# Two attentions on one core: output products one step later at the block boundary

## The chip, the cores and the metric

The kernel runs on one core of a Trainium2 chip. The metric is the device time of one execution in microseconds (us), median of several runs. Engines are named as in the profile: PE is the TensorE matmul stream and PEld its weight loads, DVE is VectorE, ACT is ScalarE, POOL is GpSimd, and SP is SyncE, whose queue issues nearly all DMAs of the main loop. L898 means line 898 of the kernel.

## The reference

Two independent multi-head attentions run over inputs of 2048 positions and 576 features, with 32 heads of 18 features. Their results stand side by side in the output.

```python
# A: local, dilated: each position looks at 8 positions, 2 apart, behind it
qkv = (x @ wqkv).reshape(B, S, 3, H, Dh).transpose(2, 0, 3, 1, 4)
logits = einsum("bhsd,bhswd->bhsw", q, kg) * Dh ** -0.5     # kg, vg: the 8 gathered keys, values
o_a = einsum("bhsw,bhswd->bhsd", softmax(masked logits), vg)
a = o_a.transpose(0, 2, 1, 3).reshape(B, S, D) @ wo_A
# B: full attention, all 2048 keys for each query
o_b = einsum("bhqk,bhkd->bhqd", softmax(q @ k^T * Dh ** -0.5), v)
b = o_b.transpose(0, 2, 1, 3).reshape(B, S, D) @ wo_B
out = concatenate([a, b], axis=-1)
```

## The kernel before

**Order.** After the projections (about the first 416 us) there is one main loop of 512 steps. It works on B: 8 groups of 4 heads, 4 blocks of 512 queries in each group, 16 key tiles of 128 keys in each block. So step s belongs to block s // 16 and key tile kt = s % 16, and a "block" below is one group with one block of queries. A step computes the scores of its key tile for four heads on PE (`score`, L388), takes their exponentials on ACT (L398 for one head, L401 for two at once), and then multiplies the exponentials of the step before it with the values, which accumulates in the PSUM tile `po` (`weigh`, L898). The values are therefore one step late: step 16n (kt = 0) holds the last value product of the block before, the one that ends it, and step 16n + 1 (kt = 1) holds the first one of the next block. When a block ends, `finish` lets DVE copy `po` to `o` (L908), and only then may the next block's first value product overwrite `po`.

**Maxima.** The softmax of B needs a bound for each query before its scores. PE computes trial products of queries and keys (L239) and DVE takes their maxima (L256, L258, L272) some blocks ahead. How many stand in a step is the planner's `many`: 3 as a rule, 2 in a kt = 1 step unless the step before it holds output products (L1388). When a block's maxima are complete, DVE reduces them once more (L282) and transposes them (L290).

**A.** Attention A runs beside the loop in eight parts j = 0 to 7, each started 55 steps after the one before (`local`, L1014). POOL does most of it; DVE takes maxima (L1059) and ACT the exponentials (L1069). A part's result goes through DRAM (`dao`), comes back in tiles `at` and `ahl` (`get`, L1118 and L1120; one buffer each), and is multiplied with `wo_A` on PE. These are the output products: for each of a part's two row tiles there are two products of 288 columns, and each takes 27 matmuls of about 0.29 us in two queues, one on each half of PE's rows, which run side by side (L1239). ACT copies the one half's sum to `y` (L1138), DVE adds the other half's (L1142).

**Where a product stands.** The list `TURNS` (L56) holds the steps in which an output product may stand. `local` takes the next two free turns for each row tile, puts them in the set `producing`, plans the tile's `get` up to 9 steps ahead of the first, and plans the store of the finished rows 5 steps after the second:

```python
TURNS = sorted({NT * n + AT for n in range(1, 30)} | {A_FROM + GAP * j + 35 for j in range(NJ)} | set(MORE))
one = next(t for t in TURNS if t >= at + 7)
two = next(t for t in TURNS if t > one + 1)
pieces.append((max(at + 1, one - 9) - start, lambda n=n: get(n)))
```

A step with products carries two maxima more than `many`, uses seven PSUM banks as one pool instead of five and a pair, and PE's order in it is made by `in_turn` (L1245) from estimated times: the two queues alternate as their estimates say, and a bank is taken when DVE or ACT is expected to have emptied it. Other steps with three maxima follow the fixed order `PLAIN`.

**Queues.** Everything a step does beside this is called at its end from an agenda. The agenda gives the order in which an engine receives instructions, not a time: SP runs ahead of PE wherever nothing it must wait for stands in front. In SP's order stand, one step after a block's end, the store of the denominators (`den`, L932, which must wait for the copy `o`), and at the start of each group the loads of the queries and keys of the group two ahead (`qs`, `ks` from `dqk`, L215 and L216; twelve loads over six steps from the group's second step on), into one of three sets of tiles, which is free when the last scores that read it are done.

Of the kernel before, what the change touches and what calls it, by code (L numbers as in the profile page):

```python
# [40 lines left out]
EARLY_PAIRS = EARLY * NB * PIECES + 8  # L41
AHEAD = 7

AT = 0

MORE = (439, 441, 451, 467, 475, 477, 484, 486)

# [7 lines left out]

TURNS = sorted({NT * n + AT for n in range(1, 30)} | {A_FROM + GAP * j + 35 for j in range(NJ)} | set(MORE))  # L56

# [12 lines left out]
def two_attentions(ctx: ExitStack, tc, xa, wa, woa, xb, wb, wob, out):  # L70
# [45 lines left out]
    def pooled(apart_):  # L116

        nonlocal ring
        ring = "pool"
        n = 7 if apart_ else 5  # L120
        if apart_:
            pair_room()
            freed[5] = freed[6] = freed["pair"]
        rings.update({k: list(range(n)) for k in ("pool", "scores", "else")})

    def apart():

        nonlocal ring
        ring = "else"
        assert not held  # L130
        if len(rings["else"]) == 7:
            pair_room()
            freed["pair"] = max(freed[5], freed[6])
        n = sorted(range(5), key=lambda i: freed[i])
        rings["scores"] = [n[1], n[3]]
        rings["else"] = [n[0], n[2], n[4]]
# [44 lines left out]
    step = 0  # L181
# [8 lines left out]
    def due():  # L190
        for f in agenda.pop(step, []):
            f()
# [126 lines left out]
    given = [0, 0]  # L319
    projecting = True  # L320

    def maximum(r):

        given[r] += 1
        return blocks[find(lambda rest: rest[r])][1](r)
# [14 lines left out]
    def first_part(r):  # L340

        for i in range(2):
            given[i] += 0.5
        if open_parts:
            part, args = open_parts.pop()
        else:
            rest, _, part = blocks[find(lambda rest: rest[0] and rest[1] and rest[0][-1][0] > 1)]
            piece = rest[0].pop()
            assert rest[1].pop() == piece
            args = (0, *piece)  # L350
            open_parts.append((part, (1, *piece)))
        ps = bank()
        ins, _ = part(*args, r, ps)
        taken = rings[ring][-1]

        def second():
            if ring == "else":
                rings["else"].remove(taken)
                rings["else"].append(taken)
            return part(*args, 1 - r, ps, ins)[1]  # L360

        return second
# [7 lines left out]
    def score(g, b, kt, h, kind):  # L370

        assert (g, b) in placed
        qs, ks = sets[g % 3]
        p, r = divmod(h, 2)
        at = slice(64 * r, 64 * r + 56)
        if len(scored) == 4:
            scored.clear()
            counted[0] += 1
        parity = counted[0] % 2
        n = sum(k == kind for k in scored)  # L380
        scored.append(kind)
        if kind == "pair":
            if n == 0:
                both_scores[:] = [pair_of_banks()]
            ps = both_scores[0][:, 512 * n : 512 * n + 512]
        else:
            ps = bank("else" if projecting else "scores")
        nc.tensor.matmul(ps, ks[at, p, 128 * kt : 128 * kt + 128], qs[at, b, p], start=True, stop=True)  # L388
        filled(r, 226, ps if kind != "pair" else None if n else both_scores[0])
        if kind == "single":  # L390
            e = whole = (work if parity else e_room).tile([128, 512], F32, name=f"e{n}{parity}", bufs=1)
        else:
            if n == 0:
                both_es[:] = [e_room.tile([128, 1024], F32, name=f"ee{parity}", bufs=1)]
            whole = both_es[0]
            e = whole[:, 512 * n : 512 * n + 512]
        if kind != "pair":
            nc.scalar.activation(e, ps, AF.Exp, scale=SCALE)  # L398
            emptied("ACT", 490, r, ps)
        elif n:  # L400
            nc.scalar.activation(whole, both_scores[0], AF.Exp, scale=SCALE)  # L401
            emptied("ACT", 916, r, both_scores[0])
        return e
# [102 lines left out]
    def do_all(fs):  # L506
        for f in fs:
            f()
# [6 lines left out]
    with (tc.tile_pool(name="x", bufs=1, side="right") as xp,  # L515
# [367 lines left out]
        step = 0  # L883
# [106 lines left out]
    producing = set()  # L990
# [254 lines left out]
    def in_turn(queues):  # L1245

        while any(queues):
            at = []
            for r, q in enumerate(queues):
                need = q[0][0] if q else None  # L1250
                free = 0
                if need == "E":
                    free = parted_at[0]
                elif need == "pair":
                    free = 0 if "pair" in held else freed["pair"] + 165
                elif need:
                    free = min(freed[i] for i in rings[ring] if i not in held) + 165 if any(i not in held for i in rings[ring]) else 1e9
                at.append(max(busy[r], free) if q else 2e9)
            r = int(at[1] < at[0])
            busy[0], busy[1] = max(busy[0], at[r]), max(busy[1], at[r])  # L1260
            queues[r].pop(0)[1]()
# [109 lines left out]
    total = early + rest  # L1371

    def behind():

        most = 0
        for n in range(int(sum(given)) // (2 * PIECES), NG * NB):
            until = NT * n - AHEAD
            more = 3 * (until - step) + 2 * sum(step <= p < until for p in producing)
            most = max(most, 2 * PIECES * (n + 1) - int(sum(given)) - more)
        return most  # L1380
# [4 lines left out]
    while step < ALL:  # L1385
        n, kt = divmod(step, NT)
        g, b = divmod(n, NB)
        many = min(4 if behind() > 0 else 2 if kt == 1 and step > 1 and step - 1 not in producing else 3, total - int(sum(given)))  # L1388
        if open_parts and total - int(sum(given)) < 3:
            many = 1  # L1390
        es = [None] * 4
        products = inside.pop(0)() if inside else ([], [])
        plain = many == 3 and not any(products)
        if not plain:
            pooled(any(products))
        parts = many == 3 or many == 1 and open_parts
        left = many - parts
        a = left // 2 if left != 1 or given[0] >= given[1] else 1
        b_ = left - a
        extra = any(products) and int(sum(given)) + many + 2 <= total  # L1400
        ops = {"D": lambda: parted.append(first_part(0)) or parted_at.insert(0, busy[0] + 250), "E": lambda: parted.pop()()(),
               "A": lambda: maximum(0)(), "B": lambda: maximum(1)(),
               "+": lambda: None,
               **{c: lambda h=i % 4, kind="single" if i < 4 else "apart" if any(products) else "pair": es.__setitem__(h, score(g, b, kt, h, kind))
                  for i, c in enumerate("0123wxyz")}}

        def queue(text, own):
            q = []
            for c in text:
                if c == "+":  # L1410
                    q += own
                    own = []
                elif c == "p":
                    q += own[:1]
                    own = own[1:]
                else:
                    q.append((c if c == "E" else "pair" if c in "wxyz" and not any(products) else True, ops[c]))
            return q

        if plain:  # L1420
            do_all(ops[c] for c in PLAIN)
        elif any(products):
            in_turn([queue(ROWS[0].replace("D", "D" * parts).replace("A", "A" * min(a, 1)).replace("X", "A" * extra), products[0]),
                     queue(ROWS[1].replace("E", "E" * parts).replace("B", "B" * min(b_, 1)).replace("X", "B" * extra), products[1])])
        else:
            in_turn([queue("D" * parts + "0y" + "A" * a, []), queue("x" + "E" * parts + "B" * b_ + "3", [])])
        for fs in (behind_scores, outside):
            while fs:
                fs.pop(0)()

        if not plain and not paired and int(sum(given)) < total:
            apart()
        paired = paired or kt % 2 == 0 and int(sum(given)) == total
        for _ in range(1 if paired and step < ALL - 2 else len(waiting)):
            if waiting:
                waiting.pop(0)()
        if ready and (kt % 2 == 0 or not paired):
            weigh(ready.pop(0))
        ready.append((g, b, kt, es))
        if paired and kt % 2:  # L1440
            weigh(*ready)
            ready.clear()
        due()

        if len(waiting) > (0 if not paired else 2 if kt % 2 else len(waiting)):
            waiting.pop(0)()
        step += 1
# [24 lines left out]
```

## Time and profile before

| | |
|---|---|
| runs shown | 1588.29, 1587.92, 1584.57 us; median 1587.92 us |
| profiled execution | 1584.54 us, span 1582.7 us |
| granted TensorE clock | 0.999 |
| PE busy | 1571.9 us, 99% of the span |
| DVE busy | 1399.5 us, 88% |
| ACT busy | 1183.0 us, 75% |
| POOL busy | 966.0 us, 61% |

A window row of the profile gives a stretch's start and end, its length, and each engine's busy time in it with the number of instructions. The chain of work that ended last is given in order of time: start, length, and what ran. A row of the timeline gives start, length, engine, line, operation and how many instructions are merged in it. A step is bounded here by the end of its last value product (L898); "x8" in the chain is one step's value products.

### The profile page before, as it was taken

The page shows a single profiled execution, that of the slowest core. Times are in us where ns is not written, and L with a number is a line of the kernel's source. Part 1 is how long each engine was busy: PE and PEld are TensorE (multiplying, and loading weights), DVE is VectorE, ACT ScalarE, POOL GpSimd, SP SyncE. Part 2 cuts the span into 40 slices and gives each one's busy share as a digit, 9 for nine tenths or more (in the row PEclk, how much of TensorE's full clock was granted, in tenths as well). Part 3 has the DMA queues.
Part 4 walks back from the last instruction along what each step waited for, and adds up shares of the span by engine and source line. Part 5 has one row for each costly group of instructions (what it writes and reads, how often), then busy time and mean ns, then how long its engine had stood idle before and what let it go on. Part 6 is the DMA issues. An engine that isn't in the chain of part 4 may idle for free.

```text
span 1582.7 us, 34698 instructions
## 1 busy us (share of the span) xinstructions
PE 1571.9 (99%) x13400; PEld 949.5 (60%) x13400; DVE 1399.5 (88%) x2381; ACT 1183.0 (75%) x1916; POOL 966.0 (61%) x820
## 2 busy tenths in 40 slices
PE   9999999999999999999999999999999999999998
PEld 7999998888544444454444445444444445455776
DVE  5299999999999999999999999999999999999433
ACT  7323441211799999999998999999999999998444
POOL 2305752201267997994995995995995997940100
PEclk9999999999999999999999999999999999999999
DMA  8848964523322253253236225423613232234211
GB/s 260 222 130 210 260 183 123 161 81 93 75 56 55 64 114 95 65 139 104 58 85 170 58 67 142 96 54 105 141 56 92 67 86 79 62 124 158 85 39 61
DMA packets 190149, 173.12 MB, mean 109 GB/s; under 512 B 123120, under 2 KB 136944, under 8 KB 188256
## 3 DMA queue, kind: packets, MB, share of 16 engines
q1 hardware_dynamic: 185120, 159.36, 36.4%
q0 software_dynamic: 4032, 10.63, 3.2%
q8 instruction: 105, 1.72, 0.5%
q10 hardware_dynamic: 832, 0.92, 0.2%
q14 instruction: 60, 0.49, 0.1%
HBM read 97.47 MB, written 72.95 MB: 108 GB/s over the span
## 4 chain that ended last, share of the span: by engine, by line
PE 93%; DVE 2%; DMA 2%; issue 1%; POOL 1%; ACT 1%; SPq 0%; POOLq 0%; ACTq 0%; DVEq 0%
PE po L898 30%; PE bank L239 20%; PE bank L498 14%; PE bank L388 9%; PE bank L1239 8%; PE pair L388 7%; PE bank L424 4%; DVE mx L256 1%; DMA ks<-dqk 1%; POOL xlo L546 1%; DMA qs<-dqk 0%; DMA at<-dao 0%; DVE mx L272 0%; DVE o L908 0%; PE bank L664 0%
## 5 line engine op out<-in xcount | busy, mean ns | idle before, releaser
L239 PE MATMUL bank<-ks,qs 54*128 54x256 f32 (+1 forms) x2526 | 756.1, 373 | 1.2 <-DVE mx L256 0.5
L256 DVE TENSOR_REDUCE mx<-bank 128x1 f32<-128x512 f32 x1024 | 680.3, 684 | 60.7 <-PE bank L239 36.2
L239 PEld LDWEIGHTS bank<-ks,qs 54*128 54x128 f32 x2526 | 414.9, 184 | 427.5 <-DVE mx L272 308.3
L398 ACT ACTIVATE e<-bank 128x512 f32<-128x512 f32 x1024 | 610.9, 602 | 75.5 <-PE bank L388 68.6
L898 PE MATMUL po<-ee,v 128*19 128x512 f32 x2048 | 536.9, 599 | 1.0 <-DVE o L908 0.2
L898 PE MATMUL po<-e,v 128*19 128x512 f32 x2048 | 531.5, 599 | 0.0
L401 ACT ACTIVATE ee<-pair 128x1024 f32<-128x1024 f32 x478 | 487.5, 1020 | 0.3
L388 PE MATMUL bank<-qs,ks 56*128 56x512 f32 x1092 | 461.1, 442 | 0.0
L258 DVE TENSOR_REDUCE mx<-bank 128x2 f32<-128x512 f32 x546 | 356.1, 685 | 19.1 <-PE bank L239 6.9
L272 DVE TENSOR_REDUCE mx<-bank 128x2 f32<-128x512 f32 x478 | 326.1, 682 | 0.0
L388 PE MATMUL pair<-qs,ks 56*128 56x512 f32 x956 | 248.5, 396 | 0.0
L388 PEld LDWEIGHTS bank<-qs,ks 56*128 56x128 f32 x1092 | 194.6, 184 | 15.4 <-ACT e L398 8.3
L1090 POOL TENSOR_TENSOR pr<-lg,akv 128x1024 f32<-128x1024 f32 x72 | 157.0, 2201 | 0.6
L840 ACT ACTIVATE ohi<-bank 128x512 f32<-128x512 f32 (+1 forms) x56 | 30.6, 595 | 148.6 <-issue 126.3
L388 PEld LDWEIGHTS pair<-qs,ks 56*128 56x128 f32 x956 | 138.3, 186 | 0.0
L898 PEld LDWEIGHTS po<-ee,v 128*19 128x19 f32 x2048 | 69.8, 97 | 111.3 <-issue 107.4
L498 PE MATMUL bank<-xhi,ahi 64*128 64x512 f32 x448 | 114.6, 391 | 0.2 <-ACT ohi L843 0.2
L498 PE MATMUL bank<-xlo,ahi 64*128 64x512 f32 (+1 forms) x448 | 102.7, 392 | 0.2 <-POOL xlo L546 0.2
L498 PE MATMUL bank<-xhi,alo 64*128 64x512 f32 x416 | 101.0, 391 | 0.0
L1042 POOL TENSOR_TENSOR pr<-aq,akv 128x1024 f32<-128x1024 f32 x40 | 87.8, 2200 | 17.2 <-PE bank L239 16.0
L1092 POOL TENSOR_TENSOR pr<-pr 128x512 f32<-128x512 f32 x72 | 91.2, 1289 | 0.6
L652 POOL TENSOR_TENSOR olo<-olo,ohi 128x512 fp32r<-128x512 f32 x36 | 46.1, 1294 | 65.7 <-ACT ohi L651 61.3
(210 smaller groups left out, 2346.2 us busy)
## 6 DMA issues: line engine op xcount, KB each, us to landing
do<-n SPq DMA_DIRECT2D x28, 512.0 KB
da<-ohi SPq DMA_DIRECT2D x52, 256.0 KB
akv<-da SPq DMA_DIRECT2D x64, 175.5 KB
out<-y SPq DMA_DIRECT2D x32, 288.0 KB
qs<-dqk SPq DMA_DIRECT2D x30, 288.0 KB
ks<-dqk SPq DMA_DIRECT2D x30, 288.0 KB
at<-dao SPq DMA_DIRECT2D x64, 128.0 KB
rec<-drec SPq DMA_DIRECT2D x29, 256.0 KB
```

What stands on the lines that cost most here:

```text
L239: return nc.tensor.matmul(ps, qs[rows_, b, p, 128 * t : 128 * t + 128], ks[rows_, p, 512 * k + at : 512 * k + at + n], start=True, stop=True)
L256: nc.vector.tensor_reduce(mx[:, r, p, t, k : k + 1], ps, axis=AX.X, op=ALU.max)
L258: nc.vector.tensor_reduce(mx[:, r, p, t, 2 * k - 2 : 2 * k], ps.rearrange("q (h n) -> q h n", h=2), axis=AX.X, op=ALU.max)
L272: nc.vector.tensor_reduce(mx[:, :, p, t, 2 * k - 2 + i], ps.rearrange("q (h n) -> q h n", h=2), axis=AX.X, op=ALU.max)
L388: nc.tensor.matmul(ps, ks[at, p, 128 * kt : 128 * kt + 128], qs[at, b, p], start=True, stop=True)
L398: nc.scalar.activation(e, ps, AF.Exp, scale=SCALE)
L401: nc.scalar.activation(whole, both_scores[0], AF.Exp, scale=SCALE)
L498: nc.tensor.matmul(ps, a, b, start=start, stop=stop)
L898: nc.tensor.matmul(po[32 * i : 32 * i + 19], vs[g][:, kt, 19 * i : 19 * i + 19], es[i], start=kt == 0, stop=kt == NT - 1)
L1090: nc.gpsimd.tensor_mul(at, ap(st["lg"], (0, 2), (SUB, W), (1, SUB)), window(st["v"], n))
L1092: nc.gpsimd.tensor_add(at[:, :, :4], at[:, :, :4], at[:, :, 4:])
L1239: nc.tensor.matmul(sums_[r], a, b, start=i == 0, stop=i == len(both[r]) - 1)
```

## The change

```diff
-AT = 0
+AT = 1
...
-        many = min(4 if behind() > 0 else 2 if kt == 1 and step > 1 and step - 1 not in producing else 3, total - int(sum(given)))
+        many = min(4 if behind() > 0 else 2 if kt == 1 and step > 1 and step not in producing and step - 1 not in producing else 3, total - int(sum(given)))
```

The regular turns move from steps 16n to steps 16n + 1: from the step with the value product that ends a block to the step with the next block's first one. The second edit keeps three maxima in a kt = 1 step that holds a product. The other turns (45 + 55j and `MORE`) stay. Worked through the lines quoted above, the 32 steps with products of A are

```
before: 112 128 144 155 | 176 192 208 210 | 224 240 256 265 | 288 304 320 336
        352 368 375 384 | 400 416 430 432 | 448 451 464 467 | 475 477 484 486
after:  113 129 145 155 | 177 193 209 225 | 241 257 265 273 | 289 305 320 337
        353 369 385 401 | 417 430 439 441 | 449 451 465 467 | 475 477 484 486
```

with a part's four products between the bars. The step of a `get` moves with its product: for example from 199 to 200 (product 208, now 209), from 247 to 258 (product 256, now 265), and from 439 to 442 (product 448, now 449). Where a part's own step 45 + 55j holds no product, its exponentials are issued in two halves rather than one: that holds for steps 45 and 100 before, and for 210 and 375 as well after.

## The prediction

> **What bounds the kernel now.** I read the page first, then the chain of work that ended last, then windows over single steps.
>
> ```profile
> span 1582.7 us, 34698 instructions
> PE 1571.9 (99%) x13400; PEld 949.5 (60%) x13400; DVE 1399.5 (88%) x2381; ACT 1183.0 (75%) x1916; POOL 966.0 (61%) x820
> PE 93%; DVE 2%; DMA 2%; issue 1%; POOL 1%; ACT 1%; SPq 0%; POOLq 0%; ACTq 0%; DVEq 0%
> ```
>
> PE holds 93% of the chain: the matmuls bound the kernel, and the change neither adds nor removes one. So it can only alter how long PE waits. Thirteen plain steps in a row (275 to 287) give the length of a step in which nothing waits:
>
> ```profile
> 997.83:1023.90 26.07, 26.07 (x210) 11.50 (x210) 24.64 (x41) 26.00 (x40) 25.99 (x26) 1.00 0.46 107
> ```
>
> 26.07 / 13 = 2.005 us. Now the chain across a boundary whose kt = 0 step has products (288, then 289 and 290), and one without products (272, 273, 274):
>
> ```profile
> 1022.90 0.99 PE po L898 x8
> ...
> 1024.69 0.80 PE bank L1239 x12
> ...
> 1026.76 0.23 PE bank L388 x2
> 1026.99 0.98 PE po L898 x8
> ...
> 1028.99 0.98 PE po L898 x8
> ...
> 1031.30 0.98 PE po L898 x8
> ```
>
> ```profile
> 993.52 0.60 DVE mx L256
> 994.11 0.61 DVE o L908
> ```
>
> The value products of steps 287 to 290 start 4.09, 2.00 and 2.31 us apart: the product step is clean, kt = 1 is clean, and kt = 2 is 0.3 us too long. Without products kt = 1 itself is late: PE waits for the copy `o`, and the copy waited for the maximum in front of it. Over the run (first the windows of kt = 2 after the 19 boundaries with a product at kt = 0, 208 and 320 left out, then kt = 1 at the nine boundaries without one, each row the sum over its windows):
>
> ```profile
> sum 41.24, PE 41.24 PEld 19.36 DVE 41.16 ACT 41.18 POOL 34.00; mean PE 2.17 PEld 1.02 DVE 2.17 ACT 2.17 POOL 1.79
> sum 19.61, PE 18.62 PEld 7.63 DVE 19.61 ACT 19.59 POOL 12.97; mean PE 2.07 PEld 0.85 DVE 2.18 ACT 2.18 POOL 1.44
> ```
>
> 41.24 - 19 x 2.005 = 3.1 us, and 19.61 - 9 x 2.005 = 1.6 us: a boundary costs about 0.17 us either way, with 3 maxima and a product before it, or with 2 and none.
>
> **Why a boundary costs that, and what the move does.** DVE is the cause:
>
> ```profile
> 1023.68 0.68 DVE L258 TENSOR_REDUCE mx<-bank 128x2 f32<-128x512 f32 x1
> 1024.61 1.29 DVE L258 TENSOR_REDUCE mx<-bank 128x2 f32<-128x512 f32 x2 [0.25 <-PE bank L239]
> ...
> 1027.61 0.45 DVE L1142 TENSOR_TENSOR y<-bank,y 128x288 f32<-128x288 f32 x1
> 1028.11 0.69 DVE L908 COPY o<-po 128x512 f32<-128x512 f32 x1
> ```
>
> DVE starts an operation 0.60 us after the one before it (two maxima of 0.69 take 1.29 together). Three fill 1.80 of a plain step's 2.005, so 0.2 is spare; the copy takes 0.60 and leaves a backlog of 0.4 that PE meets at kt = 2 as a bank not yet emptied. A product step has more room. Step 288 starts at 1023.90 (the window above); its maxima start from +0.71, the addition at +3.71, and it is over at +4.16, about when the step ends. A plain step after a product elsewhere wants DVE only here:
>
> ```profile
> 1217.17 0.69 DVE L256 TENSOR_REDUCE mx<-bank 128x1 f32<-128x512 f32 x1 [0.55 <-PE bank L239]
> ```
>
> The product step before it (375) ends at 1216.59 (its window is below), so that is +0.58 into the next, or +4.68 counted from the product step's start.
>
> After the change kt = 0 is plain. Its last maximum starts 0.22 us before kt = 1 begins (1023.68 against 1023.90, the same place), so the copy runs from +0.38, the five maxima from +0.98 in place of +0.71, the addition from +3.98 to +4.43. That is before +4.68: the backlog is gone when kt = 2 begins, by a margin of 0.25 us. PE doesn't wait for the copy either: it ends at about +1.07 and the value products stand at the step's end, at +3.1 (1026.99 - 1023.90). **So the 3.1 us go**, as the first term.
>
> Does the copy slow the product step itself? No step of this trace has a product right behind a copy. One bound is the ten product steps elsewhere than kt = 0, of which the second row here is the sum; the other is step 210 (kt = 2), which has the backlog:
>
> ```profile
> 1212.48:1216.59 4.11, 4.11 (x47) 2.98 (x47) 3.97 (x7) 2.72 (x6) 0.12 (x1) 1.00 0.00 0
> ...
> sum 41.08, PE 41.08 PEld 29.64 DVE 39.64 ACT 27.46 POOL 6.11; mean PE 4.11 PEld 2.96 DVE 3.96 ACT 2.75 POOL 0.61
> ```
>
> ```profile
> 847.16:853.48 6.32, 4.59 (x48) 3.06 (x47) 4.53 (x9) 2.76 (x6) 0.00 (x0) 1.00 0.68 214
> 855.49:859.92 4.43, 4.43 (x47) 3.21 (x47) 4.15 (x8) 2.77 (x7) 2.08 (x4) 1.00 0.67 221
> ```
>
> So 4.11 to 4.43, that is 0 to +0.33 us for each of 20 products, 0 to +6.6 us; a gain I exclude, since the matmuls stay. I take 0. In step 210 a maximum from the step before still waited when the step began:
>
> ```profile
> 855.73 1.88 DVE L256 TENSOR_REDUCE mx<-bank 128x1 f32<-128x512 f32 x3
> ```
>
> It starts at 855.73, that is +0.24, and holds a bank until about +0.9, while the product queues take their two banks at about +0.8 (1024.69 - 1023.90). After the change that last maximum still starts at -0.22; the copy behind it holds no bank of the pool, and the banks of the product step's own maxima, emptied 0.27 us later, are asked for again only by its last two scores, at +2.9 (1026.76). `in_turn` adds the copy to its estimate of DVE, but its free banks at the step's start are the same, so I expect the same order.
>
> On this a rule of the Trainium skill speaks against the change: VectorE: DVE Perf Modes, The DRAIN you can't avoid, says that the next VectorE operation doesn't start until the pipe of the one before has emptied. By it the spacing would be the full 0.68, the addition would end near +5.0, past +4.68, and the 3.1 us would come back at kt = 2. The rows above, 0.60 apart with 0.68 long operations, disagree, and I go by them.
>
> **The late transfer.** Steps 208 and 210 stand out: 6.32 and 4.43 against the 4.09 of step 288. In 208 PE waits for `at`:
>
> ```profile
> 842.37 7.57 DMA at<-dao
> ```
>
> It lands at 849.94; its users, counted as in step 288, could start at 847.16 + 0.8 = 848.0. What made it late stands on SP in front:
>
> ```profile
> 811.82 1.63 SPq L216 DMA_DIRECT2D qs<-dqk  x2
> 817.72 0.61 SPq L932 DMA_DIRECT2D den<-o  x1
> ...
> 828.28 4.98 SPq L215 DMA_DIRECT2D ks<-dqk  x4
> 835.22 2.73 SPq L1118 DMA_DIRECT2D at<-dao  x2
> ```
>
> The twelve group loads stand ahead of `at`, and the store of `den` held SP back, waiting for the copy `o` behind product step 192:
>
> ```profile
> SPq L932 <- DVE mx L256: 4.8, 1, 4.8
> ```
>
> After the change the product stands in 209, 2.0 us later, and `den` leaves some 1.8 us earlier, since the copy no longer waits for a product step (4.09 - 2.0, less its 0.24 later start). If the transfers kept their times, PE would wait about 0.1 us (849.94 against 847.16 + 2.0 - 0.17 + 0.8); if they follow SP, not at all. **Term two: -2.2 us** (6.32 - 4.1). Step 210 loses its product to 225: **-0.3 us**.
>
> **What it costs.** For parts 3 and 6 the step with the exponentials (210, 375) loses its product, so they go in two halves into a busier ACT. Windows of four steps around them, first twice without a product (44 to 47, 99 to 102), then three times with one:
>
> ```profile
> sum 16.79, PE 16.79 PEld 7.51 DVE 15.96 ACT 16.71 POOL 12.31; mean PE 2.10 PEld 0.94 DVE 2.00 ACT 2.09 POOL 1.54
> sum 30.70, PE 30.70 PEld 17.09 DVE 28.48 ACT 26.22 POOL 4.89; mean PE 2.56 PEld 1.42 DVE 2.37 ACT 2.18 POOL 0.41
> ```
>
> (16.79 - 8 x 2.005) / 2 = 0.37 against (30.70 - 3 x 4.10 - 9 x 2.005) / 3 = 0.12: +0.25 each, **+0.5 us**. Part 3's maxima (L1059) then fall into plain steps at 208; one beside a boundary (step 97) costs 0.08 against the mean of its kind, 19.61 / 9 = 2.18:
>
> ```profile
> 609.69:611.95 2.26, 2.07 (x16) 0.85 (x16) 2.26 (x5) 2.26 (x4) 1.50 (x1) 1.00 0.00 0
> ```
>
> Two of them, **+0.2 us**. Step 273 gains a product and 433 loses one: nothing. The count of maxima stays, so DVE's and PE's work does. Other `get`s keep 7 to 9 steps of lead, hidden where SP isn't behind; what that is worth is a rival below. The stores of rows move with their products and nobody waits for them.
>
> **Sum.** 1584.5 - 3.1 - 2.2 - 0.3 + 0.5 + 0.2 = 1579.6 us. That stands on the profiled execution, which is like the lowest of the runs shown (1584.57); the median, 1587.92, is 3.4 higher, and nothing here tells which level the next runs take. From the median it would be 1583.0; I say 1581.2.
>
> **Rivals.**
> - *The boundary's cost stays* (the margin of 0.25 us is used up by the block's own L282 and L290, or the banks come late). Without the first term: 1582.7, or 1586.1 from the median. For it: the margin is small. Against it: 0.60 spacing in every row.
> - *The wait for `at` only moves*, since the transfers are held by their queue and not by SP: without term two, 1581.8 to 1585.2.
> - *The product queues lose their order side by side*, as in 210: up to +6.6, so 1586.2 to 1589.6, no change or nearly slower.
> - *A `get` comes too late: slower.* Place: step 258, whose `get` now stands among the loads of group 6 (steps 257 to 262) with its product at 265. From the first such load to the landing at 208 took 849.94 - 811.82 = 38.1 us; from the start of 256, when those loads may go, to the product's need are 2.0 + 4.1 + 7 x 2.005 + 0.8 = 20.9. If all twelve stood ahead, PE would wait 17.2 us: 1597. Against it: only two loads come before this `get`. It must wait for product 257 to release the tile, at about +5.3; its first issues and a landing as above (2.7 + 7.6) end at about 16. It decides once that takes 5 us longer.
>
> **Chances.** Forecast 0.55, boundary stays 0.17, wait moves 0.08, order lost 0.09, late `get` 0.06, something unseen and slower 0.05. A difference of 0.3%, 4.8 us, is about what a measurement of this kernel can tell. The forecast is 4.9 by the sum and more from the median, so nearly all of its 0.55 counts as faster, with a part of the next two: 0.60. Same 0.27, slower 0.13. The range for 8 in 10 runs from 1576.5 (all costs at zero and SP earlier throughout) to 1590 (order lost).
>
> **What would show it.** In the new profile: kt = 2 behind a product at 2.01 and not 2.17; the copy `o` 0.38 us into kt = 1, maxima 0.60 apart behind it, product steps at 4.1; step 209 near 4.1 with no wait for `at`; step 210 plain. Wrong if product steps at kt = 1 take over 4.2, if kt = 2 stays at 2.17, or if PE waits for `at` anywhere, at 265 above all.

## The result, and the profile after

| | before | after |
|---|---|---|
| median of 9 runs | 1586.03 us | 1580.71 us |
| lowest and highest | 1584.49 to 1588.29 | 1580.02 to 1584.91 |
| profiled execution | 1584.54, span 1582.7 | 1580.33, span 1578.5 |

The changed kernel takes 0.9968 of the time before, 95% interval 0.9959 to 0.9977. The forecast was 1581.2 us. The page of the changed kernel, the same rows as before:

```profile
span 1578.5 us, 34690 instructions
PE 1569.5 (99%) x13400; PEld 963.9 (61%) x13400; DVE 1397.0 (88%) x2381; ACT 1183.3 (75%) x1918; POOL 967.0 (61%) x820
PE 94%; DVE 2%; POOL 2%; issue 1%; DMA 1%; ACT 0%; ACTq 0%; DVEq 0%; POOLq 0%
```

PE is still the chain, and DMA's share of it fell from 2% to 1%. POOL's rose from 1% to 2%, which comes back below. The chain across the boundary of steps 288 to 290, where the product now stands in 289:

```profile
1019.49 0.98 PE po L898 x8
1021.49 0.98 PE po L898 x8
1025.58 0.98 PE po L898 x8
1027.59 0.98 PE po L898 x8
```

From one row to the next: 2.00 for kt = 0, 4.09 for kt = 1 with the product, 2.01 for kt = 2. Before it was 4.09, 2.00 and 2.31. Over the run, as windows: the same 19 steps kt = 2 as before, then the 20 product steps at kt = 1, then 18 of these without 209 and 241:

```profile
sum 38.08, PE 38.08 PEld 16.73 DVE 33.57 ACT 31.34 POOL 30.95; mean PE 2.00 PEld 0.88 DVE 1.77 ACT 1.65 POOL 1.63
sum 82.40, PE 82.40 PEld 59.38 DVE 82.40 ACT 56.91 POOL 71.78; mean PE 4.12 PEld 2.97 DVE 4.12 ACT 2.85 POOL 3.59
sum 73.69, PE 73.69 PEld 53.23 DVE 73.69 ACT 51.11 POOL 65.80; mean PE 4.09 PEld 2.96 DVE 4.09 ACT 2.84 POOL 3.66
```

The 19 steps went from 41.24 to 38.08 us: they are plain steps now (38.08 / 19 = 2.004). VectorE in the timeline of that boundary, where step 289 lasts from 1022.48 to 1026.57:

```profile
1022.26 0.68 DVE L256 TENSOR_REDUCE mx<-bank 128x1 f32<-128x512 f32 x1
1022.86 0.68 DVE L908 COPY o<-po 128x512 f32<-128x512 f32 x1
1023.46 1.28 DVE L256 TENSOR_REDUCE mx<-bank 128x1 f32<-128x512 f32 x2
...
1026.45 0.45 DVE L1142 TENSOR_TENSOR y<-bank,y 128x288 f32<-128x288 f32 x1
1026.81 0.24 DVE L282 TENSOR_REDUCE m<-mx 128x16 f32<-128x96 f32 x1
1027.15 0.69 DVE L256 TENSOR_REDUCE mx<-bank 128x1 f32<-128x512 f32 x1
```

The copy starts at +0.38, the maxima at +0.98, the addition at +3.97, and the first maximum of kt = 2 at +4.67, each within 0.01 us of what was forecast. Even L282 fits into the gap.

The late transfer is the other gain. Steps 208 to 210, and SP with its longest wait for `den`:

```profile
846.14:848.22 2.08, 2.08 (x19) 0.96 (x18) 2.08 (x5) 2.01 (x4) 0.00 (x0) 1.00 0.69 255
848.22:852.65 4.43, 4.43 (x47) 3.15 (x47) 4.43 (x10) 2.88 (x7) 1.70 (x3) 1.00 0.73 253
852.65:854.81 2.16, 2.16 (x18) 0.94 (x18) 2.16 (x5) 1.98 (x4) 1.29 (x1) 1.00 0.60 178
```

```profile
SPq L932 <- DVE mx L256: 2.9, 1, 2.9
```

No wait of PE for `at` is left. But step 209 takes 4.43, which no term of the prediction held, and so does one more step, in another place:

```profile
1319.25:1321.96 2.71, 2.58 (x18) 1.07 (x18) 2.71 (x6) 2.32 (x4) 2.63 (x4) 1.00 0.51 193
```

That is step 427 (kt = 11), a plain step three steps ahead of product 430. It comes back in experiment 7.

### The profile page after: what moved, and what is told of

Same layout as the page of the kernel before. It is cut to its first block, busy times and chain, and to the rows that moved or that the text cites. A ratio compares the mean times of both kernels' runs of the same rounds, so it can differ in the third digit from the quotient of the medians.

```text
span 1578.5 us, 34690 instructions
## 1 busy us (share of the span) xinstructions
PE 1569.5 (99%) x13400; PEld 963.9 (61%) x13400; DVE 1397.0 (88%) x2381; ACT 1183.3 (75%) x1918; POOL 967.0 (61%) x820
## 4 chain that ended last, share of the span: by engine, by line
PE 94%; DVE 2%; POOL 2%; issue 1%; DMA 1%; ACT 0%; ACTq 0%; DVEq 0%; POOLq 0%
PE po L898 31%; PE bank L239 19%; PE bank L498 16%; PE bank L388 9%; PE bank L1239 8%; PE pair L388 7%; PE bank L424 4%; DVE mx L256 1%; POOL pr L1045 1%; DVE mx L272 0%; DVE o L908 0%; DMA da<-ohi 0%; POOL aohi L1042 0%; DMA first<-xb 0%; DVE mx L258 0%
## 5 line engine op out<-in xcount | busy, mean ns | idle before, releaser
L398 ACT ACTIVATE e<-bank 128x512 f32<-128x512 f32 x1024 | 610.8, 602 | 73.2 <-PE bank L388 66.5
L498 PE MATMUL bank<-xhi,ahi 64*128 64x512 f32 x448 | 119.8, 390 | 0.2
L498 PE MATMUL bank<-xlo,ahi 64*128 64x512 f32 (+1 forms) x448 | 107.8, 392 | 0.2 <-POOL xlo L546 0.2
L498 PE MATMUL bank<-xhi,alo 64*128 64x512 f32 x416 | 105.7, 390 | 0.0
```

What stands on the lines that cost most here:

```text
L498: nc.tensor.matmul(ps, a, b, start=start, stop=stop)
```

## The experiments

Theory: a boundary costs what the copy adds to VectorE, and only a product step behind the copy has room for it; the wait for `at` was a second, separate gain. Rivals: the boundary's gain comes from elsewhere or from any new place; the wait only moved; a late `get` is hidden. Ratios below are to the kernel before on the same chip; a ratio is taken over all runs and need not be the quotient of two medians. Times are medians. Line numbers in some runs stand one higher, because the edit adds a line.

**1. Only the late products, in the kernel before.**

```diff
+TURNS = sorted(set(TURNS) - {208, 210} | {209, 211})
...
-        EXPS = ((34, 0, 2), (35, 1, 2)) if A_FROM + GAP * j + 35 not in producing else ((35, 0, 1),)
+        EXPS = ((34, 0, 2), (35, 1, 2)) if A_FROM + GAP * j + 35 not in producing and j != 3 else ((35, 0, 1),)
```

The second edit of the change is in it too, for step 209.

> The kernel before, with only the products of steps 208 and 210 moved to 209 and 211 (the exponentials of part 3 stay in one piece as before). Theory: the wait for `at` in 208 and the longer step 210 are a term of their own, 2.2 + 0.3 us. The product stands 2.0 us later while `den` still leaves SP late, so the transfer lands just in time: step 209 near 4.1 to 4.3, no wait for `at` above 0.3 us, ratio to before 0.9985 (-2.0 to -2.6 us). Rival, the wait only moves: step 209 stays near 6.3 and the ratio is 1.000.

Measured: 0.9988, interval 0.9979 to 0.9996 (1582.96 against 1586.04 us). Steps 209 and 211:

```profile
849.23:853.84 4.61, 4.58 (x48) 3.15 (x47) 4.61 (x11) 2.77 (x6) 1.69 (x3) 1.00 0.74 255
855.84:860.15 4.31, 4.31 (x47) 2.99 (x47) 3.92 (x7) 3.27 (x7) 2.38 (x3) 1.00 0.42 123
```

6.32 became 4.61, and the waits of PE hold no `at` any more. So 2.0 us of later place alone removes that wait. Step 209 is longer than I said, for the most part for the reason that step 209 of the changed kernel, 4.43, is (below). The other 0.2 us are a pause of PE's weight loads that the trace puts down to no engine and no transfer; whether it is a last remainder of the wait for `at` stays open. The rival falls.

**2. The late products put back, in the changed kernel.**

```diff
+TURNS = sorted(set(TURNS) - {209} | {208})
```

> The changed kernel, with the second row tile of part 1 put back to steps 208 and 210 (the next two parts' first products then stand at 225, 241, 257, 265). Theory: SP is some 2 us earlier than before because `den` no longer waits behind product step 192, so even at 208 PE waits for `at` by 0.5 us at most, and step 210 costs 0.3 us again: 0.3 to 0.9 us slower than the changed kernel, ratio to before about 0.9973. Rival, only the later place of the product helps: step 208 takes 6.0 to 6.3 again, 2.2 to 2.5 us slower than the changed kernel, ratio about 0.9983.

Measured: 0.9982, interval 0.9971 to 0.9992 (1581.82 us, 1.1 above the changed kernel's 1580.71). The times don't decide: the ratio is the rival's 0.9983, lifted by three of the eleven runs at 1585 to 1588 us, and the median stands near the theory. The trace does. Step 208, and the chain in it:

```profile
850.99:855.82 4.83, 4.39 (x47) 3.07 (x47) 4.43 (x9) 2.75 (x6) 0.00 (x0) 1.00 0.72 239
```

```profile
845.86 6.42 DMA at<-dao
```

The step takes 4.83, not 6.3, and PE waits 0.4 us for `at`, as the theory said: the transfer landed at 852.28. Counted from the end of step 191 (816.75 here, 812.77 before) that is 35.5 us where it was 37.2 before. The `den` store went 3.1 us after that end where it was 4.95. So SP, freed 1.85 us earlier, brings the transfer in 1.6 us earlier, and either part alone removes most of the wait. The gain of the two is not a sum of the two.

**3. A `get` put where it comes too late.**

```diff
-            pieces.append((max(at + 1, one - 9) - start, lambda n=n: get(n)))
+            pieces.append(((263 if (j, n) == (2, 1) else max(at + 1, one - 9)) - start, lambda n=n: get(n)))
```

> The changed kernel, with the `get` of product 265 planned at step 263, behind all twelve loads of group 6, in place of 258. The prediction's rival priced this at up to 17 us of waiting for `at` in step 265. Theory: SP issues in order, the twelve loads take it about 21 us from the start of step 256, the six transfers of `at` and the landing 13 to 16 more, the product needs them at 20.9: a wait of 12 to 17 us in step 265, ratio to before about 1.005. Rival, the place in SP's order is hidden: no wait, ratio 0.997.

Measured: 1.0057, interval 1.0039 to 1.0076 (1595.16 us). Step 265 and its chain:

```profile
972.66:990.99 18.33, 7.01 (x47) 4.88 (x47) 4.43 (x8) 3.35 (x7) 0.11 (x1) 0.63 0.74 203
```

```profile
960.50 16.92 DMA ks<-dqk
977.42 0.02 issue
977.44 7.80 DMA at<-dao
```

18.33 - 4.09 = 14.2 us more in one step, inside the 12 to 17. But not all of it is waiting: PE stands still for 18.33 - 7.01 = 11.3 us, a little less than forecast, and its matmuls take 7.01 us in place of 4.09, at a granted clock that is 0.63 on average in this step (the last section). The prediction's slower rival, 17.2 us, was of the right size; what kept it away is the order on SP, two loads in front and not twelve. This run has two executions only, 1593.08 and 1597.24 us.

**4. The copy twice, before and after.** The second copy repeats the first.

```diff
-        nc.vector.tensor_copy(o, po)
-        emptied("DVE", 598, 0, None)
+        for _ in range(2):
+            nc.vector.tensor_copy(o, po)
+            emptied("DVE", 598, 0, None)
```

> The kernel before, with `finish` copying `po` to `o` twice (the second copy repeats the first). Theory: a boundary's cost is the time that the copy takes on VectorE, and the plain steps behind it have no room left; the second copy, 0.60 us, is paid nearly in full at the 21 boundaries with a product at kt = 0 (at kt = 1 and 2) and at the 9 without one (PE waits at kt = 1): +15 to +19 us, ratio to before 1.010 to 1.012.

> The changed kernel with the same second copy. Theory: the product step at kt = 1 has about 0.25 us of room left behind the first copy, so of the second one's 0.60 us 0.35 is paid at each of the 20 boundaries and all of it at the 9 without a product and at 320: +12 to +14 us over the changed kernel, kt = 2 at 2.2 to 2.4, product steps still 4.1; ratio to before 1.004 to 1.006. Rival, the product step has no room and the boundary's gain came from somewhere else: +18, ratio 1.008.

Measured: 1.0124 (1.0108 to 1.0140; 1607.83 us, 20.7 more) before and 1.0066 (1.0048 to 1.0084; 1598.51 us, 17.8 above the changed kernel) after. Both cost more than forecast, and the second stands by its time at the rival's +18. The windows tell why. With two copies, before, the windows of kt = 1, then kt = 2, behind the same 19 product steps, then the nine kt = 1 without products:

```profile
sum 50.45, PE 39.40 PEld 16.74 DVE 48.31 ACT 39.98 POOL 42.70; mean PE 2.07 PEld 0.88 DVE 2.54 ACT 2.10 POOL 2.25
sum 42.69, PE 42.69 PEld 19.53 DVE 42.69 ACT 33.54 POOL 34.34; mean PE 2.25 PEld 1.03 DVE 2.25 ACT 1.77 POOL 1.81
sum 26.18, PE 18.61 PEld 7.60 DVE 25.87 ACT 22.18 POOL 15.36; mean PE 2.07 PEld 0.84 DVE 2.87 ACT 2.46 POOL 1.71
```

With two copies, after, the 20 product steps at kt = 1 and the 20 steps kt = 2 behind them:

```profile
sum 90.83, PE 89.67 PEld 60.49 DVE 90.14 ACT 59.16 POOL 76.45; mean PE 4.48 PEld 3.02 DVE 4.51 ACT 2.96 POOL 3.82
sum 43.13, PE 43.13 PEld 18.73 DVE 43.13 ACT 32.61 POOL 36.17; mean PE 2.16 PEld 0.94 DVE 2.16 ACT 1.63 POOL 1.81
```

And with one copy, the same kt = 1 before and the same 20 kt = 2 after:

```profile
sum 38.12, PE 38.12 PEld 16.78 DVE 36.73 ACT 30.26 POOL 35.65; mean PE 2.01 PEld 0.88 DVE 1.93 ACT 1.59 POOL 1.88
sum 40.25, PE 40.25 PEld 17.68 DVE 35.49 ACT 33.09 POOL 33.02; mean PE 2.01 PEld 0.88 DVE 1.77 ACT 1.65 POOL 1.65
```

Before, the second copy costs (50.45 - 38.12 + 42.69 - 41.24) / 19 = 0.73 us at a boundary with a product and (26.18 - 19.61) / 9 = 0.73 at one without. That is all of its time on VectorE: two copies last 1.42 us from 1042.38 on (L909), one lasts 0.69, so the second starts 0.73 after the first. The first copy costs 0.17 there, because plain steps have a little room; the second finds none left. Most of it, (50.45 - 38.12) / 19 = 0.65, shows at kt = 1 and not at kt = 2, and in another wait than the first copy's: PE may not overwrite `po` until the second copy has read it. PE's waits with two copies, before and after (us in total, times, longest):

```profile
PE po L898 <- DVE o L909: 19.7, 30, 0.9
PE po L898 <- DVE o L909: 8.1, 10, 0.9
```

So this run shows what more time in the copy costs at a boundary; that the single copy's 0.17 at kt = 2 is a backlog rests on the rows of steps 288 to 290 and on experiment 6. After, the second copy costs (90.83 - 82.40 + 43.13 - 40.25) / 20 = 0.57. The product step swallows the whole first copy, and 0.16 of the second one's 0.73. I had said 0.25 of room, and that the rest would show at kt = 2: three quarters of it shows in the product step itself, which takes 4.54 and not 4.1. The rival has the time but not the reason: for a second copy the product step has next to no room, but the first one costs nothing there.

**5. Products at kt = 2.** The edit, against the changed kernel:

```diff
-AT = 1
+AT = 2
...
-MORE = (439, 441, 451, 467, 475, 477, 484, 486)
+MORE = (439, 441, 452, 468, 475, 477, 484, 486)
...
-step not in producing and step - 1 not in producing
+step + 1 not in producing and step - 1 not in producing
```

> The regular products at kt = 2 (AT = 2), with 3 maxima in the kt = 1 step in front of a product, so that the copy's backlog meets the product step as it did in step 210 before. Theory (a maximum of the step before holds a bank that the product queues need): the 20 product steps at kt = 2 take 4.3 to 4.4 in place of 4.1, kt = 1 is clean; 4 to 6 us slower than the changed kernel, ratio to before 0.999 to 1.001. Rival (a late VectorE alone costs a product step nothing): product steps 4.1, ratio 0.997.

Measured: 1.0015, interval 1.0006 to 1.0024 (1588.44 us, 7.7 above the changed kernel). First come 21 steps kt = 1 (20 in front of a product at kt = 2, and step 385, which has 2 maxima and no product behind it; step 321, behind product 320, takes 2.03 us and is not among them), then the 21 product steps at kt = 2, and last steps 427 and 428:

```profile
sum 45.81, PE 43.87 PEld 18.70 DVE 45.81 ACT 45.50 POOL 39.72; mean PE 2.09 PEld 0.89 DVE 2.18 ACT 2.17 POOL 1.89
sum 88.63, PE 88.63 PEld 63.98 DVE 82.85 ACT 52.27 POOL 73.04; mean PE 4.22 PEld 3.05 DVE 3.95 ACT 2.49 POOL 3.48
```

```profile
1326.96:1331.06 4.10, 2.85 (x19) 1.06 (x18) 3.97 (x8) 2.56 (x4) 4.02 (x5) 0.92 0.34 125
1331.06:1334.32 3.26, 3.26 (x18) 1.50 (x18) 2.75 (x6) 2.12 (x4) 3.09 (x3) 0.58 0.51 199
```

The time came out somewhat above the 4 to 6 us, and the mechanism did not come out. kt = 1 isn't clean: 45.81 / 21 = 2.18, the 0.17 of a boundary without products, whether it holds 3 maxima or 2. Product steps average 4.22, half of what I expected on top of 4.1. So the gain is not one of "any other step": one step later it is lost again. Steps 427 and 428 take 7.36 in place of 4.78 in the changed kernel, 2.6 us of the 7.7 (experiment 7 and the last section).

**6. Two maxima at kt = 0.** At a boundary without products PE waits at kt = 1 for the copy, and the copy for the last maximum of kt = 0.

```diff
-2 if kt == 1 and step > 1 and step not in producing and step - 1 not in producing else 3
+2 if kt == 0 and step not in producing and step + 1 not in producing else 3
```

> The changed kernel, with the 2 maxima of a boundary without products given to the kt = 0 step and not the kt = 1 step. Theory: at these nine boundaries PE waits at kt = 1 for the copy, and the copy waits for the last maximum of kt = 0; with one maximum less in front the copy starts some 0.25 us earlier, and kt = 1 takes 2.0 in place of 2.17: -1.5 us, ratio to before 0.9959. Rival, the step with 2 maxima is itself the slow one: 0.9968 as for the changed kernel, the 0.17 only moves to kt = 0.

Measured: 0.9956, interval 0.9944 to 0.9969, but 1580.98 us, no less than the changed kernel's 1580.71; the kernel before stood at 1587.08 on this chip. The ratio is near the theory's 0.9959, but its interval overlaps that of the changed kernel, 0.9959 to 0.9977, so the times don't show a gain. The nine kt = 1, then the nine kt = 2 behind them:

```profile
sum 18.21, PE 18.21 PEld 8.04 DVE 17.98 ACT 18.15 POOL 10.15; mean PE 2.02 PEld 0.89 DVE 2.00 ACT 2.02 POOL 1.13
sum 19.72, PE 19.72 PEld 9.08 DVE 19.65 ACT 19.34 POOL 11.55; mean PE 2.19 PEld 1.01 DVE 2.18 ACT 2.15 POOL 1.28
```

kt = 1 is clean (18.21 in place of 19.59 in the changed kernel), and kt = 2 pays instead (19.72, there 18.07). Together the two take 37.93 in place of 37.66. Theory and rival both missed: the wait went from kt = 1, but not to kt = 0; the backlog came in its place, at kt = 2. Among these plain steps the copy is only passed on.

**7. Step 427.** The chain of the changed kernel there:

```profile
1314.43 2.39 POOL pr L1045
...
1316.90 1.30 POOL lg L1049
...
1318.23 0.40 DVE am L1059
1318.62 0.60 DVE mx L258
1319.22 0.61 DVE mx L272
...
1319.88 0.50 PE bank L239
```

GpSimd ends part 7's logits late, VectorE waits for them with its maxima queued behind, and PE waits for a bank. From part 6's first maxima (step 370) to the planned ones of part 7 (step 425) PE took 119.7 us before, with products at 375, 384, 400 and 416 in between, and GpSimd, from the first maxima to the end of the logits, as much. Now only 385, 401 and 417 lie there: PE would be through in 117.2, and GpSimd takes 117.8. One product more in that stretch:

```diff
+TURNS = sorted(set(TURNS) - {433} | {423})
```

> The changed kernel with turn 423 added and 433 taken out, so that products 439 and 441 become 423 and 439 (parts 5: 417, 423, 430, 439). Theory: step 427 waits 0.7 us because GpSimd comes late with part 7's logits, since only three product steps (before: four) stand between steps 370 and 425 while it works them off; with a fourth one again the wait of step 427 falls below 0.2 us: -0.5 to -0.7 us, ratio to before 0.9964. Rival, the place of products doesn't matter to GpSimd: step 427 stays near 2.7.

Measured: 0.9951, interval 0.9938 to 0.9963 (1580.00 us, beside the same 1587.08). Step 427:

```profile
1321.49:1323.50 2.01, 2.01 (x19) 0.89 (x18) 2.01 (x5) 2.01 (x4) 1.93 (x3) 1.00 0.53 196
```

2.71 became 2.01, as the theory said. The changed kernel did not run on this chip, so only the trace shows this gain.

**8. That version with 321 as well, beside the changed kernel.**

```diff
+TURNS = sorted(set(TURNS) - {320, 433} | {423})
```

> The changed kernel once more, as the mark for the next one on the same chip: ratio to before 0.996 to 0.997.

> The version with products 423 and 439, and product 320 moved behind the copy as well, to 321. Theory: 0.6 to 0.7 us less at 427 and 0.1 to 0.2 less around 320 than the changed kernel, so about 0.8 us below it: ratio to before 0.9957 to 0.9965, hardly to be told from the changed kernel by its time alone; in the trace steps 322 at 2.01 and 427 near 2.0.

Measured: 0.9973 (0.9964 to 0.9983) for the changed kernel again, 1581.21 us, and 0.9968 (0.9956 to 0.9980) for the version, 1580.22 us. Both lie just above what was expected. Steps 322 and 427 take 1.99 and 2.02, as expected. The two intervals overlap: by time this version is not shown to be faster than the changed kernel. Against the kernel before it is.

## Why the prediction was right, and where it was off

- *PE bounds, the change alters only waits*: right. The profiled executions differ by 4.2 us, of which 3.5 lie between steps 2 and 486, 0.5 ahead of the main loop, where the code is the same, and 0.2 behind.
- *First term, the boundary, -3.1*: right, in place and size. -3.2 measured (41.24 to 38.08), with each VectorE start of steps 289 and 290 as forecast. Experiments 4 to 6 show the cause: the copy's time on VectorE, and of the three places tried for a product (kt = 0, 1 and 2) room for it only in the product step directly behind it. What the second edit of the change is worth by itself no run shows. The rule of the Trainium skill (VectorE: DVE Perf Modes, The DRAIN you can't avoid), that the next operation waits for an empty pipe, would have brought the cost back; the after trace again has starts 0.60 apart with 0.68 long operations. That section of the Trainium skill itself adds that an operation which nothing holds starts earlier, which I had left out: these rows behave as that exception.
- *The product step keeps its 4.1*: right for 18 of 20. The margin, 0.25 by the working, was 0.16 by experiment 4. Step 209 shows the failed case: two more VectorE instructions of part A and of the block's end (L1059 and L290) stand behind the copy there, the maxima start at +1.65 in place of +0.98, and the step takes 4.43.

```profile
848.85 0.68 DVE L908 COPY o<-po 128x512 f32<-128x512 f32 x1
849.45 0.38 DVE L1059 TENSOR_REDUCE am<-lg 128x16 f32<-128x128 f32 x1
849.75 0.20 DVE L290 STREAM_TRANSPOSE mt<-m 128x32 f32<-128x32 f32 x1
849.87 1.25 DVE L256 TENSOR_REDUCE mx<-bank 128x1 f32<-128x512 f32 x2
```

  So the cost that I gave the place of the maxima at 208, +0.2 for two of them, was mis-sized: steps 208 to 210 together stand 0.07 + 0.34 + 0.16 above 2.01, 4.09 and 2.00. Step 241 took 4.28 for another reason: its maxima start at +0.97 (918.08, the step from 917.11), but a weight load of its product waits 0.2 us for an exponential of ACT (L398).
- *The bank as the cause of step 210*: open. The term, -0.3, came, since 210 is a plain step now; but in experiment 5 the product steps that meet a backlog grew by half of it or less on average. That test met the condition only in part: in its step 290 the last maximum of the step before starts at +0.00 (1028.41), in 210 it started at +0.24. Where a product step is much too long, in 209 and in experiment 4, its own maxima start late.
- *Second term, the wait for `at`, -2.2*: right, and each of the two reasons given for it removes most of the wait alone (experiments 1 and 2). No run tells how they share the 2.2.
- *Costs, +0.7*: too small. The exponentials in halves came as priced around 375 (steps 374 to 377: 0.37 above plain steps, before 0.16 with the product's 4.10 taken off); around 210 they can't be told from step 209. Left out was GpSimd: taking product 375 out of the stretch from 370 to 425 made it the bound at step 427, +0.6. I had looked at who waits for a product, not at who lives on the time that a product step gives.
- *The sum*: -4.9 forecast, -4.2 between the profiled executions and -5.3 between the medians. In the steps of the main loop it is -3.5: -3.2 for the boundary, -2.0 for steps 208 to 210 (with product 210 now in 225), +0.6 for step 427, and +1.0 net over all others. Of this +1.0, four plain steps (122, 269, 358 and 445) hold 0.2 each, in which a score waits 0.2 us for a bank that an exponential of ACT (L398) has not emptied; why there, no run shows. So the costs were too small by more than GpSimd's part. That the number, 1581.2, still came within 0.5 us of the median, 1580.71, is partly luck: the gain was counted 1.4 us too high, and the kernel before stood at 1586.03 over nine runs, 1.5 above the profiled execution that the sum starts from. The choice between the two levels of the runs shown was a guess that turned out near.
- *The rivals*: the late `get` is worth 14 us (experiment 3) and didn't come; the boundary's cost didn't stay; the wait didn't move; a product step as long as 210 came once, in 209.

## What to carry to other kernels

In this kernel a short extra operation on a second engine costs what exceeds the little room of the steps around it, and moving it among full steps only moves the wait. It cost nothing directly in front of the step in which the bounding engine is busy with work that the other doesn't feed. When such a step is moved, look at three things beside its own waits: what stood in a queue behind the old place (a store on SP that held twelve loads and a transfer back), what other small instructions meet it at the new place, and which engine lived on the time that the step took where it was. A product step moved out of a stretch shortened it for PE by 2.5 us, and GpSimd, whose work there had just fitted before, became late (0.7 us at step 427).

## What was not expected of the hardware

In experiment 5 PE stands still for about 1.2 us at the start of step 427 (1327.0 to 1328.1), and some 2 us later the granted TensorE clock falls to half for about 3.4 us:

```profile
1327.00:1328.00 1.00, 0.00 (x0) 0.00 (x0) 0.91 (x3) 0.41 (x1) 1.00 (x2) 1.00 0.00 0
1328.00:1329.00 1.00, 0.78 (x4) 0.47 (x6) 1.00 (x3) 0.34 (x1) 0.92 (x3) 1.00 0.00 0
...
1330.00:1331.00 1.00, 1.00 (x10) 0.01 (x2) 1.00 (x3) 1.00 (x2) 1.00 (x2) 0.71 0.58 211
1331.00:1332.00 1.00, 1.00 (x9) 1.00 (x7) 0.63 (x2) 0.25 (x2) 0.92 (x2) 0.50 0.06 25
```

Step 428 takes 3.26 in place of 2.07 for it, so the stall is paid a second time. The Trainium skill (TensorE: Matmul & The Clock Gate, What's actually happening) describes a gate that halves the clock after about 3.4 us of idleness in a free-running window; the stall here is shorter. The long wait of experiment 3, 11.3 us, fits it, with a granted clock of 0.50 from about 980 to 990. Two waits in step 208 don't settle where the limit lies: in the kernel before PE stood still for 1.1 and then 0.6 us, and the clock stayed at full; with two copies (experiment 4, before) it stood still for 1.6 and then 0.5 us, and the clock was 0.79 on average over the step's 8.10 us. What decides between them no run here shows.
